# The first chunk of an input weight loaded and rounded while the batch's rows still arrive

## The chip, the cores and the metric

The kernel runs on one core of a Trainium2 chip. A core has TensorE (matrix products; the trace gives its matmuls as PE and its weight loads as PEld), VectorE (DVE), ScalarE (ACT), GpSimd (POOL) and SyncE (SP), which here issues most of the DMAs. Every engine works through its own list of instructions in order; semaphores tie the lists together. DMAs issued by SP and by ScalarE stand in two queues and share the core's 16 transfer engines. The metric is the device time of one execution in microseconds.

## The reference

```python
def _attn_ref(x):                       # x: (8, 3008, 256) f32
    X = np.fft.fft(x, axis=1)
    X = np.fft.fft(X, axis=2)
    return X.real.astype(np.float32)

def _moe_ref(x, w_in, w_out):           # (24064, 256), (256, 2048), (2048, 256)
    h = x @ w_in
    g = h * (1.0 / (1.0 + np.exp(-1.702 * h)))
    return (g @ w_out).astype(np.float32)
```

The result of the first is reshaped to 24064 rows and handed to the second. In the kernel `w_in` and `w_out` come as 64-bit floating-point values, seen as pairs of 32-bit words, and are rounded to 32 bits on the chip.

## The kernel before

The Fourier transform along the 3008 rows is split as 47 x 64. The first stage (`fold_first`, `mix_first` for batch 0; `fold1`, `mix1` for the others) combines 47 rows each, the second (`stage2`) 64. The transform along the 256 columns is folded into `w_in`: `fold_w(n)` multiplies a rounded chunk of `w_in` by cosines and sines and leaves `wcs[0]` and `wcs[1]`. So each inner step only multiplies `pq`, the result of the second stage, by `wcs`, applies the activation and multiplies by `w_out`. There are 384 steps, numbered by batch, block, half and pair. Steps 0 to 7 use plain products (`hidden(t)`, `rows(t)`, `activate(t)`, `product(t)`), while the weights are still being rounded; from step 8 on a scheme with fewer products and more sums runs, which needs differences of the rounded `w_out`.

The order of the instructions is written out by hand (`tc.manual_schedule()`), so the order of the calls is the order on each engine. The change lies in what happens before step 0, L834 to L902:

- SP loads the table `w0` in two parts (L836, L841) and batch 0's x in four pairs of row groups (`load_first(0)` to `load_first(3)`, L266, four, three, three and three DMAs). A pair holds groups `g` and `7-g` of four row slots each. Then it loads raw chunk 0 of `w_in` (`load_in(0)`, 1024 KB), the tables `small`, and raw chunk 1. At most eight of these DMAs are in flight; each semaphore is waited for before it is used again.
- `odd_weights` (L280) makes a second table from `w0` on ScalarE. `fold_first(g)` (L288, L290) folds a group on VectorE; `mix_first(i)` (L308) multiplies on TensorE and copies the result out on ScalarE (L310). After every second one `spill_first` stores the first 16 rows to `Td` in DRAM by two DMAs, one on SP's and one on ScalarE's queue (L314); the others follow later on SP. `fill` (L336) reads `Td` back as `t`, turned.
- The rounding of a raw chunk has six kinds of instruction: `squares` (L406 on ScalarE, or L408 on VectorE), `clamp` (L411, GpSimd), `low_up` (L416) and `low_down` (L421) on ScalarE, `high` (L438, L439, L440, VectorE) and `finish_in` (L452, GpSimd; `finish_out`, L460, for `w_out`), which leaves `wst`.
- `fold_w` (L182 as `psw`) takes 16 matmul passes on TensorE and two copies on ScalarE (L479). `first_row` (as `psf`) needs both copies. `rotate` (as `psr`, copy L343) and `stage2` (L356, transposes L362 on VectorE) need `t` and leave `pq`. `nyquist` (as `psn`, copy L374) makes `nb`, which `rows` needs. `warm(n)` is n matmuls without a use.

Before the change chunk 0 is rounded behind the seventh `mix_first` and later, partly in halves of 512 elements, with its squares on VectorE; `fold_w(0)`, `first_row(0)`, `rotate`, `stage2(0, 0)` follow, and `fold_w(1)` comes after `stage2`. `load_out(0)` stands on ScalarE's queue.

Of the kernel before, what the change touches and what calls it, by code (L numbers as in the profile page):

```python
# [46 lines left out]
def view(ap, offset, *dims):  # L47
    return bass.AP(ap.tensor, ap.offset + offset, [list(d) for d in dims])


def free(ap, offset, *dims):
    return bass.AP(ap.tensor, ap.offset + offset, [list(ap.ap[0])] + [list(d) for d in dims])
# [58 lines left out]
def kernel(ctx: ExitStack, tc, x, w_in, w_out, tab1, tab2, out):  # L111
    nc = tc.nc
# [43 lines left out]
    def ring(tag):  # L156
        at, size, count = rings[tag]
        i = turns[tag] = turns.get(tag, -1) + 1
        return big[:, at + i % count * size:at + (i % count + 1) * size]
# [7 lines left out]
    def bank(name, tag=None):  # L167
        if tag is None:
            tag = spare.pop(0)
            spare.append(tag)  # L170
        if tag in ("o0", "o1"):
            return o_banks[int(tag[1])]
        return (rest if tag[0] == "o" else psp).tile([128, 512], F32, tag=tag, name=name)
# [5 lines left out]
    def halves(out, lhs, rhs, **how):  # L179

        for c0 in (0, 64):
            nc.tensor.matmul(out[c0:c0 + 64], lhsT=lhs[:, c0:c0 + 64], rhs=rhs, skip_group_check=True, **how)  # L182
# [86 lines left out]
    def load_first(k):  # L269

        lo, two_ = 4 * k, (((28 - 8 * k) * D, 2), (1, 4 * D))
        load_rows(0, lo, lo, two_, two_)
        for at in lo, 28 - lo:
            skip = at == 0
            load_rows(1, at + skip, NB - at - skip, ((D, 4 - skip), (1, D)), ((-D, 4 - skip), (1, D)))
        if k == 0:
            load_rows(1, 0, NJ, ((1, D),), ((1, D),))

    def odd_weights(lo, hi):
        nc.scalar.activation(odd[:, lo:hi], w0[:, lo:hi], ACTF.Copy, scale=w0[:, n0:n0 + 1])  # L280
# [11 lines left out]
    def mix_first(i):  # L292

        ps, ns = bank("ps1"), (2 * i + 2, 2 * i + 1) if i < 7 else (0, 15)
        for at, n in enumerate(ns):
            todo = [], []
            for c, slot in enumerate((n, NJ - n if n else 16)):
                o = ps[64 * c:64 * c + 64, at * D:(at + 1) * D]
                even, odd_ = (w[:, k * NM:k * NM + 64] for w, k in ((w0, slot), (odd, slot or NJ)))
                todo[c].append((o[:, H + 1:], odd_, room[slot // 4][:, slot % 4, 0:H - 1], True, True))  # L300
                folded = slot // 4 not in BY_PE
                todo[c].append((o[:, 0:H + 1], even, xt[:, slot, 0:H + 1], True, folded))
                if not folded:
                    todo[c].append((o[:, 1:H], even, free(xt[:, slot], D - 1, [-1, H - 1]), False, True))
            for k in range(3):
                for c in range(2):
                    for o, w, rhs, first_, end in todo[c][k:k + 1]:
                        nc.tensor.matmul(o, lhsT=w, rhs=rhs, start=first_, stop=end, skip_group_check=True)  # L308
        to = 2 - i % 2 * 2
        nc.scalar.copy(made[i // 2][:, to:to + 2, :].rearrange("p j d -> p (j d)"), ps[:])  # L310
# [11 lines left out]
    def warm(n):  # L322

        ps = bank("warm")
        for _ in range(n):
            nc.tensor.matmul(ps[:], lhsT=wcs[0][:, 0:128], rhs=wcs[0][:, 0:512], start=True, stop=True)
# [59 lines left out]
    def load_in(n, eng):  # L386
        t = raw["in", n] = ring("raw").bitcast(U32).rearrange("p (n w) -> p n w", w=2)
        eng.dma_start(out=t[:].rearrange("p (i f) w -> p i (f w)", i=2),
                      in_=w_in[:, n * 512:(n + 1) * 512].bitcast(U32).rearrange("(i p) f -> p i f", p=128))

    def load_out(n, eng):
        t = raw["out", n] = ring("raw").bitcast(U32).rearrange("p (n w) -> p n w", w=2)
        eng.dma_start(out=t[:].rearrange("p (f n) w -> p f (n w)", f=4),
                      in_=w_out[4 * n * 128:(4 * n + 4) * 128, :].bitcast(U32).rearrange("(p f) n -> p f n", p=128))
# [3 lines left out]
    def prepare(key):  # L398


        pre[key] = ring("s"), ring("m"), ring("r").bitcast(U32)

    def squares(key, eng):
        g, hi = pre[key][0], raw[key][:, :, 1].bitcast(F32)
        if eng is nc.scalar:
            eng.activation(g[:], hi, ACTF.Square)  # L406
        else:
            eng.tensor_tensor(g[:], hi, hi, op=ALU.mult)  # L408

    def clamp(key, lo=0, n=1024):  # L410
        nc.gpsimd.tensor_scalar(pre[key][1][:, lo:lo + n], raw[key][:, lo:lo + n, 1].bitcast(F32), scalar1=TOP, scalar2=-TOP,  # L411
                                op0=ALU.min, op1=ALU.max)

    def low_up(key, lo=0, n=1024):

        nc.scalar.activation(pre[key][2][:, lo:lo + n].bitcast(F32), raw[key][:, lo:lo + n, 0], ACTF.Copy, scale=2.0 ** -29,  # L416
                             bias=2.0 ** 23)

    def low_down(key, lo=0, n=1024):
        r = pre[key][2][:, lo:lo + n]  # L420
        nc.scalar.activation(r, r.bitcast(F32), ACTF.Copy, bias=-2.0 ** 23)  # L421
# [8 lines left out]
    def high(key, lo=0, n=1024):  # L430

        g, m, _ = (t[:, lo:lo + n] for t in pre[key])
        bits = m.bitcast(U32)
        if lo == 0:
            made_a[key] = ring("a").bitcast(U32)
        a = made_a[key][:, lo:lo + n]
        dve = nc.vector
        dve.scalar_tensor_tensor(m, g, LOW * LOW, m, op0=ALU.is_ge, op1=ALU.mult)  # L438
        dve.tensor_scalar(a, bits, scalar1=3, scalar2=0x3FFFFFF8, op0=ALU.logical_shift_left, op1=ALU.bitwise_and)  # L439
        dve.scalar_tensor_tensor(a, bits, 0xC0000000, a, op0=ALU.bitwise_and, op1=ALU.bitwise_or)  # L440
# [5 lines left out]
    def finish_in(n, lo=0, k=1024):  # L446

        if lo == 0:
            wst[n] = op.tile([128, 2, 512], F32, tag="os", name="wst")
        key, part = ("in", n), slice(lo, lo + k)  # L450
        out = wst[n][:].rearrange("p i f -> p (i f)")[:, part]
        nc.gpsimd.tensor_tensor(out.bitcast(U32), made_a[key][:, part], pre[key][2][:, part], op=ALU.add)  # L452
# [19 lines left out]
    def fold_w(n):  # L472
        ps = [bank("psw") for _ in range(2)]
        for i in range(2):
            for cs in range(2):
                halves(ps[cs][:], cd[:, i, cs, :], wst[n][:, i, :], start=(i == 0), stop=(i == 1))
        for cs in range(2):

            nc.scalar.copy(wcs[cs][:, n * 512:(n + 1) * 512].rearrange("p (f c) -> p f c", f=4),  # L479
                           free(ps[cs][:], 0, [1, 4], [4, 128]))  # L480
# [346 lines left out]
    for i, pair_of in enumerate(((0, 7), (1, 6), (2, 5), (3, 4))):  # L827
        for k, g in enumerate(pair_of):
# [6 lines left out]
    ends = n0 + 4 - 28 * NM  # L835
    nc.sync.dma_start(out=free(w0, 0, [28 * NM, 2], [1, ends]),  # L836
                      in_=view(tab1, 0, [tab1.shape[1], 128], [28 * NM, 2], [1, ends]))
    for i in range(4):
        load_first(i)
        if i == 0:  # L840
            nc.sync.dma_start(out=w0[:, ends:28 * NM], in_=tab1[:, ends:28 * NM])  # L841
    load_in(0, nc.sync)
    nc.sync.dma_start(out=small[:], in_=tab2)
    load_in(1, nc.sync)
    odd_weights(NM, ends)
    odd_weights(28 * NM, n0)
    odd_weights(ends, 28 * NM)
    warm(6)

    in0, in1, out0, in2 = ("in", 0), ("in", 1), ("out", 0), ("in", 2)  # L850
    prepare(in0)
    for i, need in enumerate(((0, 7), (1,), (6,), (2,), (5,), (3,), (4,), ())):
        for g in need:
            fold_first(g)
        mix_first(i)
        if i % 2:
            spill_first(i // 2, 0, 16, (nc.sync, nc.scalar))
        if i == 6:
            low_up(in0, 0, 512)
            low_down(in0, 0, 512)  # L860
            squares(in0, nc.vector)
            for h0 in (0, 512):
                clamp(in0, h0, 512)
            for h0 in (0, 512):
                high(in0, h0, 512)
    load_out(0, nc.scalar)
    low_up(in0, 512, 512)
    low_down(in0, 512, 512)
    fill(0, 0, 4)
    load_in(2, nc.sync)  # L870
    for k in range(4):
        spill_first(k, 16, NM, (nc.sync, nc.sync))
    prepare(in1)
    squares(in1, nc.scalar)
    finish_in(0, 0, 512)
    clamp(in1)
    finish_in(0, 512, 512)
    low_up(in1)
    low_down(in1)
    for h0 in (0, 512):  # L880
        high(in1, h0, 512)
    load_out(1, nc.sync)
    fill(0, 4, NG)
    warm(1)
    fold_w(0)
    warm(1)
    first_row(0)
    prepare(out0)
    for h0 in (0, 512):
        finish_in(1, h0, 512)  # L890
    clamp(out0)
    rotate(0, 0, 4, nc.scalar.copy)
    squares(out0, nc.scalar)
# [4 lines left out]
    high(out0)  # L898
    load_in(3, nc.sync)
    prepare(in2)  # L900
    fold_w(1)
    finish_out(0)  # L902

    extra, early = {}, {}
# [166 lines left out]
```

## Time and profile before

| | |
|---|---|
| time, median of 4 runs | 1861.51 us (1860.86 to 1862.45) |
| profiled execution | 1860.86 us, its span 1859.1 us |
| busy in the span | PE 1840.7, PEld 1400.9, DVE 1519.7, ACT 1145.2, POOL 964.2 us |
| mean granted clock of TensorE | 0.997 |
| SP issues raw chunk 0 / chunk 1 | 13.62 / 15.09 us |
| last `mix_first` copied out | 22.44 + 0.57 us |
| `fold_w(0)`, `stage2(0, 0)`, `fold_w(1)` begin on TensorE | 26.43, 33.68, 35.83 us |
| `hidden(0)` begins | 39.31 us |

An "idle before, releaser" in brackets is the time that the engine stood still before that instruction, and what ended it. A wait for several semaphores is put down to the last. The chain of waits follows the work that ended last back to the start. The table of stretches gives each engine's busy time in chosen parts of the span, then the granted clock as a share of the full one, the transfer engines' busy share and what they moved.

### The profile page before, as it was taken

The page shows a single profiled execution, that of the slowest core. Times are in us where ns is not written, and L with a number is a line of the kernel's source. Part 1 is how long each engine was busy: PE and PEld are TensorE (multiplying, and loading weights), DVE is VectorE, ACT ScalarE, POOL GpSimd, SP SyncE. Part 2 cuts the span into 40 slices and gives each one's busy share as a digit, 9 for nine tenths or more (in the row PEclk, how much of TensorE's full clock was granted, in tenths as well). Part 3 has the DMA queues.
Part 4 walks back from the last instruction along what each step waited for, and adds up shares of the span by engine and source line. Part 5 has one row for each costly group of instructions (what it writes and reads, how often), then busy time and mean ns, then how long its engine had stood idle before and what let it go on. Part 6 is the DMA issues. An engine that isn't in the chain of part 4 may idle for free.

```text
span 1859.1 us, 56025 instructions
## 1 busy us (share of the span) xinstructions
PE 1840.7 (99%) x23700; PEld 1400.9 (75%) x23700; DVE 1519.7 (82%) x2222; ACT 1145.2 (62%) x2239; POOL 964.2 (52%) x1048
## 2 busy tenths in 40 slices
PE   8999999999999999999999999999999999999998
PEld 4577777777777777777777777777777777778776
DVE  6888788888788877987789878888888888878874
ACT  5656665666666556666665666656666666656663
POOL 3676345844367443773348643486445754434442
PEclk9999999999999999999999999999999999999999
DMA  9721340225112240113302232031411111100111
GB/s 320 162 60 35 78 74 19 65 54 98 23 30 60 62 89 19 52 45 88 63 13 57 52 86 52 17 77 34 101 31 25 36 46 36 31 18 13 22 20 24
DMA packets 150315, 106.36 MB, mean 57 GB/s; under 512 B 106041, under 2 KB 131161, under 8 KB 149488
## 3 DMA queue, kind: packets, MB, share of 16 engines
q1 hardware_dynamic: 148704, 101.20, 23.8%
q8 instruction: 187, 3.06, 0.7%
q10 hardware_dynamic: 1360, 1.57, 0.3%
q14 instruction: 64, 0.52, 0.1%
HBM read 65.46 MB, written 48.05 MB: 61 GB/s over the span
## 4 chain that ended last, share of the span: by engine, by line
PE 91%; DVE 2%; DMA 2%; POOL 2%; ACT 1%; issue 1%; SPq 0%; DVEq 0%; POOLq 0%; ACTq 0%
PE x L182 33%; PE o L182 25%; PE low L669 24%; PE o L669 4%; PE ps L253 2%; PE ps L356 1%; ACT x L576 1%; POOL big L606 0%; POOL big L607 0%; DMA big<-in_moe_w_in_dram 0%; DVE big L635 0%; PE po L182 0%; DMA t<-Td 0%; DVE big L549 0%; DMA xt<-in_x_dram 0%
## 5 line engine op out<-in xcount | busy, mean ns | idle before, releaser
L606 POOL TENSOR_TENSOR big<-big 128x256 f32<-128x256 f32 (+1 forms) x376 | 347.9, 925 | 829.3 <-ACT big L598 711.2
L182 PE MATMUL x<-pq,wcs 128*64 128x256 f32 (+1 forms) x6016 | 771.3, 377 | 1.3 <-ACT x L576 0.5
L635 DVE TENSOR_TENSOR big<-big 128x512 f32<-128x512 f32 (+1 forms) x736 | 624.7, 863 | 30.6 <-PE low L669 14.4
L182 PE MATMUL o<-big,wo 128*64 128x256 f32 (+1 forms) x4800 | 621.1, 375 | 0.0
L182 PEld LDWEIGHTS x<-pq,wcs 128*64 128x64 f32 x6016 | 410.3, 137 | 190.8 <-issue 15.0
L182 PEld LDWEIGHTS o<-big,wo 128*64 128x64 f32 x4800 | 342.2, 137 | 147.1 <-DVE big L613 0.5
L588 ACT ACTIVATE g<-x 128x512 f32<-128x512 f32 (+1 forms) x376 | 221.6, 589 | 375.2 <-PE x L182 374.1
L549 DVE TENSOR_TENSOR big<-g,x 128x512 f32<-128x512 f32 (+2 forms) x440 | 253.7, 588 | 197.5 <-ACT big L591 197.1
L669 PE MATMUL low<-big 128*64 128x128 f32 (+1 forms) x5888 | 382.8, 270 | 0.0
L576 ACT ACTIVATE x<-nb,af 128x256 f32<-128x256 f32 (+1 forms) x752 | 352.8, 469 | 12.2
L669 PEld LDWEIGHTS low<-big 128*64 128x64 f32 x5888 | 337.6, 137 | 29.2
L607 POOL TENSOR_TENSOR big<-big 128x256 f32<-128x256 f32 (+1 forms) x376 | 358.7, 954 | 0.0
L591 ACT ACTIVATE big<-x 128x512 f32<-128x512 f32 (+1 forms) x376 | 220.4, 586 | 196.2 <-PE x L182 165.5
L598 ACT ACTIVATE big<-big 128x512 f32<-128x512 f32 (+1 forms) x376 | 231.9, 617 | 40.0 <-DVE big L549 38.0
L669 PE MATMUL low<-big,wo 128*64 128x128 f32 (+1 forms) x2944 | 220.2, 270 | 0.1
L669 PEld LDWEIGHTS low<-big,wo 128*64 128x64 f32 x2944 | 171.6, 137 | 3.2 <-DVE big L635 0.4
L614 DVE TENSOR_TENSOR big<-big 128x512 f32<-128x512 f32 (+1 forms) x188 | 157.6, 839 | 6.5
L613 DVE TENSOR_TENSOR big<-big 128x512 f32<-128x512 f32 (+1 forms) x188 | 136.8, 728 | 5.5 <-POOL big L606 5.5
L770 DVE TENSOR_TENSOR big<-big,low 128x512 f32<-128x512 f32 (+3 forms) x184 | 109.1, 610 | 3.5
L669 PEld LDWEIGHTS o<-big,wo 128*64 128x64 f32 x1472 | 92.3, 137 | 24.9
L669 PE MATMUL o<-big,wo 128*64 128x128 f32 (+1 forms) x1472 | 110.0, 270 | 0.0
L225 POOL TENSOR_TENSOR xt<-xt 111x510 f32<-111x510 f32 x56 | 82.3, 1469 | 4.4
(92 smaller groups left out, 953.4 us busy)
## 6 DMA issues: line engine op xcount, KB each, us to landing
out_dram<-os SPq DMA_DIRECT2D x284, 64.0 KB
t<-Td SPq DMA_DIRECT2D x22, 512.0 KB
Td<-xt SPq DMA_DIRECT2D x56, 192.0 KB
xt<-in_x_dram SPq DMA_DIRECT2D x18, 512.0 KB
xt<-Xr SPq DMA_DIRECT2D x14, 512.0 KB
nb<-Nd SPq DMA_DIRECT2D x23, 256.0 KB
out_dram<-os SPq DMA_DIRECT2D x96, 56.0 KB
Xr<-in_x_dram SPq DMA_DIRECT2D x7, 752.0 KB
```

Of the source, the lines that this page charges most:

```text
L182: nc.tensor.matmul(out[c0:c0 + 64], lhsT=lhs[:, c0:c0 + 64], rhs=rhs, skip_group_check=True, **how)
L549: nc.vector.tensor_tensor(free(out, at + m - 1, [by, 2], [RUN, blocks], [-1, m]), *ins, op=op)
L576: nc.scalar.activation(x[:, i * 256:i * 256 + n], nbt[b, blk][:, hh * 256:hh * 256 + n], ACTF.Copy, scale=af1[:, f:f + 1])
L588: nc.scalar.activation(two(g[:], n), two(xb[t][:], n), ACTF.Copy, scale=2.0)
L591: nc.scalar.activation(front(t), two(xb[t][:], width(t)), ACTF.Gelu_apprx_sigmoid)
L598: nc.scalar.activation(back(t), back(t), ACTF.Gelu_apprx_sigmoid)
L606: eng.tensor_tensor(right(t, S1, n), left(t, A21, n), right(t, A22, n), op=ALU.add)
L607: eng.tensor_tensor(left(t, S3, n), left(t, A11, n), left(t, A21, n), op=ALU.subtract)
L613: eng.tensor_tensor(s2, s1, a11, op=ALU.subtract)
L614: eng.tensor_tensor(s4, a12, s2, op=ALU.subtract)
L635: nc.vector.tensor_tensor(out, i0, i1, op=how)
L669: nc.tensor.matmul(o, lhsT=lhs, rhs=rhs, start=first_in, stop=(p == NP - 2), skip_group_check=True)
```

## The change

Raw chunk 0 is loaded right behind x's first pair, ahead of the second part of `w0` and of x's other three pairs. Its squares, `low_up`, `low_down` (ScalarE) and `clamp` (GpSimd) are issued in one piece ahead of the last `odd_weights`; its `high` and `finish_in` stand behind the first `mix_first`. `load_out(0)` is issued by SP, behind the stores after the sixth `mix_first`. The warm-up matmul ahead of `fold_w(0)` is gone, and `fold_w(1)` comes ahead of `rotate` and `stage2(0, 0)`.

```diff
+    in0, in1, out0, in2 = ("in", 0), ("in", 1), ("out", 0), ("in", 2)
     for i in range(4):
         load_first(i)
         if i == 0:
+            load_in(0, nc.sync)
             nc.sync.dma_start(out=w0[:, ends:28 * NM], in_=tab1[:, ends:28 * NM])
-    load_in(0, nc.sync)
     nc.sync.dma_start(out=small[:], in_=tab2)
     load_in(1, nc.sync)
     odd_weights(NM, ends)
     odd_weights(28 * NM, n0)
+    prepare(in0)
+    squares(in0, nc.scalar)
+    low_up(in0)
+    low_down(in0)
+    clamp(in0)
     odd_weights(ends, 28 * NM)
     warm(6)
 
-    in0, in1, out0, in2 = ("in", 0), ("in", 1), ("out", 0), ("in", 2)
-    prepare(in0)
     for i, need in enumerate(((0, 7), (1,), (6,), (2,), (5,), (3,), (4,), ())):
         for g in need:
             fold_first(g)
         mix_first(i)
+        if i == 0:
+            high(in0)
+            for h0 in (0, 512):
+                finish_in(0, h0, 512)
         if i % 2:
             spill_first(i // 2, 0, 16, (nc.sync, nc.scalar))
-        if i == 6:
-            low_up(in0, 0, 512)
-            low_down(in0, 0, 512)
-            squares(in0, nc.vector)
-            for h0 in (0, 512):
-                clamp(in0, h0, 512)
-            for h0 in (0, 512):
-                high(in0, h0, 512)
-    load_out(0, nc.scalar)
-    low_up(in0, 512, 512)
-    low_down(in0, 512, 512)
+        if i == 5:
+            load_out(0, nc.sync)
     fill(0, 0, 4)
     load_in(2, nc.sync)
     for k in range(4):
         spill_first(k, 16, NM, (nc.sync, nc.sync))
     prepare(in1)
     squares(in1, nc.scalar)
-    finish_in(0, 0, 512)
     clamp(in1)
-    finish_in(0, 512, 512)
     low_up(in1)
     low_down(in1)
     for h0 in (0, 512):
         high(in1, h0, 512)
     load_out(1, nc.sync)
     fill(0, 4, NG)
-    warm(1)
     fold_w(0)
     warm(1)
     first_row(0)
     prepare(out0)
     for h0 in (0, 512):
         finish_in(1, h0, 512)
+    fold_w(1)
     clamp(out0)
     rotate(0, 0, 4, nc.scalar.copy)
     squares(out0, nc.scalar)
     stage2(0, 0)
...
     high(out0)
     load_in(3, nc.sync)
     prepare(in2)
-    fold_w(1)
     finish_out(0)
```

## The prediction

> **What bounds the kernel now.** I read the page first, then the timeline of the first 50 us engine by engine, then the chain of waits there, and last the table of stretches for the granted clock.
>
> The page's chain says what a change at the start can be worth:
>
> ```profile
> PE 91%; DVE 2%; DMA 2%; POOL 2%; ACT 1%; issue 1%; SPq 0%; DVEq 0%; POOLq 0%; ACTq 0%
> PE x L182 33%; PE o L182 25%; PE low L669 24%; PE o L669 4%; PE ps L253 2%; PE ps L356 1%; ACT x L576 1%; POOL big L606 0%; POOL big L607 0%; DMA big<-in_moe_w_in_dram 0%; DVE big L635 0%; PE po L182 0%; DMA t<-Td 0%; DVE big L549 0%; DMA xt<-in_x_dram 0%
> ```
>
> From about 62 us on TensorE sets the time, and the change does not touch that work. Whatever it does happens before the first inner steps; what counts is when these start, and a shift there moves the end by as much. The marker I use is VectorE's first instruction of `rows(1)`. The timeline leads up to it (start us, us, engine, line; in brackets the idle time before and its releaser):
>
> ```profile
> 11.68 0.69 DVE L288 TENSOR_TENSOR first<-xt 128x508 f32<-128x508 f32 x1 [1.00 <-DMA xt<-in_x_dram]
> 20.54 1.23 DVE L408 TENSOR_TENSOR big<-big 128x1024 f32<-128x1024 f32 x1 [1.98 <-DMA big<-in_moe_w_in_dram]
> 26.15 1.13 ACT L406 ACTIVATE big<-big 128x1024 f32<-128x1024 f32 x1
> 33.77 1.28 POOL L452 TENSOR_TENSOR wst<-big 128x512 uint32<-128x512 uint32 x1 [1.09 <-DVE big L440]
> 35.83 3.65 PE L182 MATMUL psw<-wst,small 128*64 128x512 f32 x16
> 39.31 1.03 PE L182 MATMUL pa<-pq,wcs 128*64 128x256 f32 x8
> 42.26 0.59 ACT L374 COPY nb<-psn 128x512 f32<-128x512 f32 x1 [1.28 <-PE psn L182]
> 45.96 0.57 ACT L520 COPY v<-pa 128x512 f32<-128x512 f32 x1
> 46.55 0.69 DVE L558 TENSOR_TENSOR big<-v,pb 128x512 f32<-128x512 f32 x1 [2.07 <-ACT v L520]
> ```
>
> Read upward: 46.55 waited for ScalarE's copy, that for the rounding of chunk 2 behind the copy of `nb` at 42.26, that for TensorE: `hidden(0)` at 39.31 plus two 1.0 us groups. `hidden(0)` stood behind the second transform (35.83), whose operand GpSimd finished at 33.77 + 1.28 = 35.05. So before, both raw chunks, loaded after x, are rounded between 20.54 and 35.05, and this serial work sets the pace.
>
> The chain shows the price of a store on ScalarE's queue with and without SP's loads in flight:
>
> ```profile
> 17.90 6.06 DMA Td<-big
> 24.03 2.19 DMA Td<-e
> ```
>
> The table of stretches (busy us per engine, then granted clock, DMA share, GB/s) shows the clock and the loads:
>
> ```profile
> 9.36:12.77 3.41, 1.90 (x20) 1.14 (x18) 2.35 (x5) 1.78 (x2) 0.00 (x0) 1.00 1.03 386
> 12.77:16.19 3.42, 3.14 (x30) 3.05 (x30) 3.31 (x6) 0.58 (x1) 0.00 (x0) 0.50 1.06 380
> 23.01:26.43 3.42, 0.00 (x0) 0.00 (x1) 3.32 (x5) 1.49 (x4) 1.63 (x2) 1.00 0.80 199
> 26.43:29.84 3.41, 3.41 (x8) 0.76 (x8) 3.34 (x4) 2.94 (x3) 2.70 (x2) 0.50 0.93 353
> ```
>
> The loads run at 380 to 400 GB/s without a gap until about 24 us. TensorE is granted half its clock in the stretch after one in which it was idle, or busy for 1.90 of 3.41 us.
>
> **The change part by part.** Times are of the profiled execution (span 1859.1, 1.8 around it, 1860.86 in all, 0.65 under the median 1861.51).
>
> *Chunk 0 loaded behind x's first pair.* 1024 KB ahead of the rest of `w0` and x's other three pairs: at 380 to 400 GB/s 2.6 to 2.8 us. The fold that started at 11.68 has its data at 14.4. The load is moved past 10 DMAs on SP's queue (the rest of `w0`, nine of x); they wait for it in the transfer engines, and the total up to chunk 1 is the same bytes, so `small` and chunk 1 land as before (chunk 1 about 25.2: ScalarE and GpSimd use it at 26.15 and 26.35 with no wait of theirs for it).
>
> *Chunk 0 rounded while x arrives.* It lands near 10.7 (the first fold ran at 7.95, then 1024 KB). ScalarE: three passes of 1024 elements as in the rows of chunk 1, 1.13 + 1.14 + 1.06, until 14.1; ScalarE has only the 1.20 us `odd_weights` to do behind it, before its first copies. GpSimd's clamp 1.30, until 12.1. VectorE's three instructions cost 1.18 + 0.69 + 1.23 = 3.1 (rows at 36.25 to 39.4), so 12.1 to 15.3. Their cover is the wait for x, now 2.7 longer; it ends at 14.4, so 0.9 shows. GpSimd's two adds (1.57 each) are done by 18.5, beside the folds. What goes in exchange: the squares on VectorE (1.23 at 20.54), twelve half-size instructions on VectorE and GpSimd, four on ScalarE, all between 20.5 and 30.
>
> *First stage of batch 0.* VectorE's folds took 11.68 to 18.56 in one piece; now 15.3 to 22.2, x's pairs coming at the same 2.7 us. TensorE ended 3.15 behind them (21.71) because it ran at half clock to 16.19. In the later start the half-clock stretch falls on the first folds, and it has two groups of about 0.9 left after the last fold: 24.0 to 25.3, I take 24.2. Bounds: no shift beyond x's 2.7, or the old lag in full.
>
> *First transform straight behind it.* No warm-up matmul, no wait for GpSimd: 16 matmuls, 3.45, 24.2 to 27.7. But its copies (L479) stand on ScalarE behind chunk 1's three passes, and `warm(1)` and `first_row(0)` wait for these copies.
>
> *Chunk 1 on ScalarE.* Ahead of it stands the last store on ScalarE's queue, which waits for the second one's landing. The second was issued at 17.90; now 3.1 later, at 21.0. With loads in flight it takes up to 6.06, without 2.19: 23.2 to 27.1. Before it landed with the loads of the time, so I take 26.1, near the upper row. L406 then starts at 26.4 (before 26.15), the passes end at 29.7. Chunk 1's own landing bounds it below at 25.3.
>
> [...]
>
> *Chunk 1 on VectorE and GpSimd.* Before, it waited for chunk 0 until 28.13. Now it starts at 27.6: first half 0.68 + 0.43 + 0.69, second 0.68 + 1.38 + 0.69 (the 1.38 is the row beside a running GpSimd, 0.43 that without); GpSimd's halves at 29.7 and 32.2, done at 33.8, 1.25 earlier than before.
>
> *Second transform, now ahead of `rotate` and stage 2.* TensorE: copy L479 done at 30.3 and 30.9, warm-up, `psf` to 31.9. At full clock it needs 1.72 per half, the second half from 33.8: end 35.5. TensorE is idle from 27.7 to 30.3, in a stretch that may grant half afterwards; half clock over one stretch of 3.4 ends it at 37.0. The start of the kernel shifts against these stretches, so I take the middle, 36.3.
>
> [...]
>
> *Stage 2.* It comes after the transform instead of before it. `rotate`'s copy now stands behind two L479 on ScalarE: 0.7 + 0.2. Then the second half of stage 2 (0.6), and the transposes (1.44), which were hidden under the second transform and now stand bare: `hidden(0)` at 36.3 + 2.9 = 39.2, against 39.31. `high(out0)` moves behind the transposes, 39.4 to 42.5, and `rows(0)` with it to 42.6; its row had 2.07 of idle time after it, which covers this. `finish_out(0)` ends near 45, before the first product (49.78).
>
> *`load_out(0)` on SP instead of ScalarE.* It stands ahead of the last store of the first 16 rows on SP, and takes 2.7. That store lands near 29.4 instead of 25 to 26, and the first read of `t` (26.37 before, used at 33.47 without a wait, so at most 7.1 long) is issued at 29.5 and is there between 33 and 36.5. Stage 2 wants it at 36.3: hidden, with nothing to spare at the upper end. ScalarE's queue loses 0.49 of issuing.
>
> *Sum.* The operand of the second transform: chunk 1's start +0.25, one chunk less in VectorE's and GpSimd's way -1.5, so 33.8 for 35.05. From there to `hidden(0)` it was 4.26; now it is 1.72 + 0.8 for the clock + 2.9 = 5.4, so +1.15. Together -0.1: median 1861.51 - 0.1 = 1861.4.
>
> **The rivals.** *Faster:* the store lands before chunk 1 (L406 at 25.4), GpSimd does not slow VectorE, TensorE stays at full clock: the transform runs through from 30.9 to 34.4, `hidden(0)` at 36.95, 2.35 earlier: 1859.2. For it: each row exists at the low value. Against: all three are needed.
>
> *Slower:* ScalarE's store waits out the whole SP queue, which now holds `load_out(0)` too. Its bytes are in at 27.2; with 2.19 the second store lands at 29.4, L406 starts at 29.75, 3.35 later than in my sum, and the longer gap on TensorE (27.7 to 33.5) puts the whole first half of the transform at half clock: 36.3 becomes 40.4, and the time 1865.5. It decides from a landing at about 29. For it: 6.06. Against: SP issues that load only near 23.3, 2.3 after the store.
>
> *Hidden:* the shift is absorbed where the chain touches GpSimd, between 107 and 125 us (`big`, `xt`): 1861.5 whatever happens before. Against: VectorE has no idle time in its rows from 46.55 to 64, TensorE works on from there, and GpSimd waits for their results.
>
> *The change does not do what it says* if chunk 0 lands after x's second pair; against that is the queue order, which has it behind 1.3 MB only.
>
> **How the numbers follow.** About 0.2% (3.7 us) is what a measurement of this kernel can tell from no change. My case (within 1.5 of the median): 0.5. Faster rival and what lies towards it: 0.2, of which 0.06 goes under -3.7 (something that I have as serial is not). Slower rival and towards it: 0.25, of which 0.16 reaches +3.7 (the store, a late `t`, or the clock on top). Hidden: 0.05. So faster 0.06, same 0.78, slower 0.16. Range: 1858.8 (under the faster rival) to 1865.6 (the slower one), leaving out about 2 in 10.
>
> **What would show it.** Right: VectorE's `high` of chunk 0 between two folds near 12 to 15; first stage ending near 24; L406 of chunk 1 near 26.4; last L452 of chunk 1 near 33.8; `hidden(0)` at 39 +- 1; `rows(1)` at 46.5. Wrong: L406 after 28 (store), a stretch at 0.50 around 31 to 37 longer than one (clock), `psr` waiting for `t` (read), or folds slowed beside GpSimd's adds.

## The result and the profile after

The changed kernel takes 1865.09 us (median of 38 runs, 1863.58 to 1866.73) against 1861.43 for the kernel before (58 runs on the same chips, 1860.72 to 1864.01). The ratio is 1.0018, 95% interval 1.0014 to 1.0023: slower by 3.66 us. I forecast no change, 1861.4. The profiled execution of the changed kernel took 1864.27, its span is 1862.4 (before 1859.1).

The chain of the page looks as before, with TensorE in nearly all of it (92% for 91%). So the place to look is again the start. The timeline of the changed kernel (start us, us, engine, line, operation; in brackets the idle time before and its releaser), the lines that answer to those of before, and the folds; other rows are left out:

```profile
11.65 1.13 ACT L406 ACTIVATE big<-big 128x1024 f32<-128x1024 f32 x1 [7.11 <-DMA big<-in_moe_w_in_dram]
...
12.89 1.23 DVE L438 SCALAR_TENSOR_TENSOR big<-big 128x1024 f32<-128x1024 f32 x1 [2.16 <-POOL big L411]
...
16.02 0.68 DVE L288 TENSOR_TENSOR first<-xt 128x508 f32<-128x508 f32 x1
16.26 3.23 POOL L452 TENSOR_TENSOR wst<-big 128x512 uint32<-128x512 uint32 x2 [3.45 <-DVE big L440]
16.73 1.63 DVE L290 TENSOR_TENSOR xt<-xt 128x508 f32<-128x508 f32 x1
18.29 1.75 DVE L288 TENSOR_TENSOR first<-xt 128x508 f32<-128x508 f32 x1
20.07 0.69 DVE L290 TENSOR_TENSOR xt<-xt 128x508 f32<-128x508 f32 x1
...
23.32 1.28 DVE L288 TENSOR_TENSOR big<-xt 128x508 f32<-128x508 f32 x2
...
28.95 1.17 ACT L406 ACTIVATE big<-big 128x1024 f32<-128x1024 f32 x1 [0.44 <-ACT e L310]
...
34.91 1.27 POOL L452 TENSOR_TENSOR wst<-big 128x512 uint32<-128x512 uint32 x1 [1.09 <-DVE big L440]
...
34.42 3.75 PE L182 MATMUL psw<-wst,small 128*64 128x512 f32 x16
...
40.84 1.08 PE L182 MATMUL pa<-pq,wcs 128*64 128x256 f32 x8 [0.20 <-DVE pq L362]
...
48.14 0.69 DVE L558 TENSOR_TENSOR big<-v,pb 128x512 f32<-128x512 f32 x1 [1.82 <-ACT v L520]
...
67.92 1.08 PE L182 MATMUL pb<-pq,wcs 128*64 128x256 f32 x8 [0.50 <-DVE t L343]
...
1237.36 0.29 PE L253 MATMUL ps<-e,w 47*64 47x129 f32 x1 [0.50 <-DVE big L549]
```

Chunk 0 lands at 11.65 and is rounded before the second pair of x is folded, as the change says. Then two folds that take 0.69 alone take 1.63 and 1.75 while GpSimd makes chunk 0's two adds (16.26 to 19.49). The last fold ends at 24.60 (before 18.56). ScalarE's squares of chunk 1 start at 28.95 (before 26.15), the last add of chunk 1 ends at 36.18 (before 35.05), `hidden(0)` starts at 40.84 (before 39.31), `rows(1)` at 48.14 (before 46.55). So 1.59 us are lost when the inner steps start. The line at 67.92 is a second loss: a `pb` matmul waits 0.50 us for VectorE's copy L343. The line at 1237.36 is a third: TensorE waits 0.50 us for VectorE in the first stage of a later batch. Before, the rows that answer to these two stand without a bracket:

```profile
65.65 1.03 PE L182 MATMUL pb<-pq,wcs 128*64 128x256 f32 x8
...
66.10 0.16 DVE L343 COPY t<-psr 128x8 f32<-128x8 f32 x1
...
1234.78 0.32 PE L253 MATMUL ps<-e,w 47*64 47x129 f32 x1
```

There `pb` started 0.45 ahead of that copy. After it the changed kernel is 2.3 us behind instead of 1.6. Near 920 us it wins back 0.3, and at the wait of 1237.36 it loses 0.7, which makes 2.7 up to TensorE's last matmul; the rest of the 3.3 between the spans lies behind that. The wait at 1237 us stands in the traces of all four kernels that keep `high(in0)` behind the first `mix_first` (the changed one and three of those below) and in none of the other nine traces. What ties it to that place is not shown.

The chain of waits of the changed kernel (start us, us, what; steps of issuing are left out) names the work that sets the end of the first part:

```profile
16.73 1.65 DVE xt L290
18.42 9.47 PE ps L308 x122
27.92 0.59 ACT e L310
28.54 0.36 ACTq L314
28.95 1.17 ACT big L406
```

It runs from the slowed fold through TensorE's first stage, then ScalarE's last copy, the issue of the store, and the squares of chunk 1. The store is issued without a wait; what holds the squares is the first stage. In the same kernel's stretches (busy us of PE, PEld, DVE, ACT, POOL, with instructions, then granted clock, DMA share, GB/s):

```profile
12.77:16.19 3.42, 0.00 (x0) 0.00 (x0) 3.23 (x4) 3.39 (x5) 0.04 (x1) 0.50 1.07 389
16.19:19.60 3.41, 1.87 (x16) 1.47 (x17) 3.38 (x3) 0.26 (x1) 3.23 (x2) 0.50 1.07 380
19.60:23.01 3.41, 3.41 (x32) 2.91 (x30) 3.31 (x6) 1.17 (x2) 0.00 (x0) 0.53 1.03 411
...
29.84:33.25 3.41, 1.92 (x9) 0.66 (x6) 2.93 (x5) 3.37 (x5) 0.89 (x1) 1.00 0.45 183
33.25:36.66 3.41, 3.41 (x28) 1.22 (x28) 1.54 (x2) 0.24 (x2) 2.32 (x3) 1.00 0.71 226
```

TensorE is idle in the first of them and at half clock for nearly all of the first three, so the first stage has two suspects: the folds and the clock. In the second transform (34.42) the clock is full (1.00).

### The profile page after: what moved, and what is told of

The parts are those of the page before. It is cut to its first block, busy times and chain, and to the rows that moved or that the text cites. A ratio compares the mean times of both kernels' runs of the same rounds, so it can differ in the third digit from the quotient of the medians.

```text
span 1862.4 us, 56008 instructions
## 1 busy us (share of the span) xinstructions
PE 1839.3 (99%) x23698; PEld 1401.5 (75%) x23698; DVE 1516.9 (81%) x2218; ACT 1145.5 (62%) x2238; POOL 961.9 (52%) x1047
## 4 chain that ended last, share of the span: by engine, by line
PE 92%; DVE 3%; ACT 2%; issue 1%; POOL 1%; DMA 0%; SPq 0%; ACTq 0%; DVEq 0%; POOLq 0%
PE x L182 34%; PE o L182 25%; PE low L669 24%; PE o L669 4%; PE ps L253 2%; PE ps L356 1%; DVE big L635 1%; PE ps L308 1%; ACT x L576 0%; DVE big L549 0%; DMA big<-in_moe_w_in_dram 0%; PE psw L182 0%; DVE big L770 0%; PE po L182 0%; DVE big L438 0%
## 5 line engine op out<-in xcount | busy, mean ns | idle before, releaser
L606 POOL TENSOR_TENSOR big<-big 128x256 f32<-128x256 f32 (+1 forms) x376 | 348.1, 926 | 829.9 <-ACT big L598 704.4
```

The costliest lines, as they stand in the source:

```text
L606: eng.tensor_tensor(right(t, S1, n), left(t, A21, n), right(t, A22, n), op=ALU.add)
```

## The experiments

Theory A: the delay at the start comes from the folds, which start late behind `high(in0)` and which GpSimd's adds slow by 2.0 us (0.94 and 1.07 in the two rows above). Theory B: it comes from TensorE's half clock. Theory C, for the wait at 67.92: one of the two warm-ups is gone, and with it one turn of the six rotating PSUM banks (`spare`, which `bank()` takes from the front and puts back at the end), so that every later tile sits in the next bank and one of them meets a reader that is not done. Times are compared with the kernel before on the same chip (1861.2 to 1861.3).

**The bank alone, in the changed kernel.** One turn of the banks is put in the place of the removed warm-up.

```diff
+    spare.append(spare.pop(0))
     fold_w(0)
```

> The changed kernel with the PSUM banks turned on by one place ahead of fold_w(0), as the removed warm-up matmul did; no instruction is added. Bank theory: the matmul group pb of hidden(5) no longer waits for VectorE's copy of rotate (0.50 of PE idle at 67.92 in the changed kernel), the step from +1.59 to +2.32 us between 65 and 70 us goes, and the time falls by 0.7 to about 1864.4. Rival, that this step belongs to the loads of batch 1 or to the later start: no change, 1865.1.

Measured: 1863.98, ratio 1.0012 [1.0003, 1.0021], with `hidden(0)` at 40.68 and `rows(1)` at 47.97. The timeline of this kernel has the same `pb` without a wait:

```profile
67.08 1.03 PE L182 MATMUL pb<-pq,wcs 128*64 128x256 f32 x8
...
67.52 0.16 DVE L343 COPY t<-psr 128x8 f32<-128x8 f32 x1
```

It starts ahead of the copy again. The distance to the trace of before stays at 1.4 between 60 and 75 us, where the changed kernel goes from 1.6 to 2.3. C holds, and the delay at the start is untouched by it.

**The bank alone, in the kernel before.** The same warm-up is taken out there, nothing else.

```diff
-    warm(1)
     fold_w(0)
```

> The kernel before with the warm-up matmul ahead of fold_w(0) taken out and nothing else. Bank theory: TensorE's pb of hidden(5) waits for VectorE's copy of rotate as in the changed kernel, a step of +0.7 us between 65 and 70 us, 1862.1. Rival, that the banks only matter with the later start: no change, 1861.4.

Measured: 1862.44, ratio 1.0006 [0.9997, 1.0015]. The time alone would not decide; the timeline does:

```profile
66.28 1.08 PE L182 MATMUL pb<-pq,wcs 128*64 128x256 f32 x8 [0.51 <-DVE t L343]
66.05 0.16 DVE L343 COPY t<-psr 128x8 f32<-128x8 f32 x1
```

`rows(1)` is at 46.44, 0.11 earlier than before, and after this `pb` the kernel is 0.67 behind. So the wait needs no early load; dropping the warm-up makes it.

**Chunk 0's adds out of the folds' way.** In the changed kernel the two adds of GpSimd go behind the clamp of chunk 1.

```diff
         if i == 0:
             high(in0)
-            for h0 in (0, 512):
-                finish_in(0, h0, 512)
...
     clamp(in1)
+    for h0 in (0, 512):
+        finish_in(0, h0, 512)
```

> The changed kernel with GpSimd's two adds of chunk 0 put behind the clamp of chunk 1, so that GpSimd stands still while VectorE folds. Theory that the adds slow the folds: the two folds that took 1.63 and 1.75 take 0.69, the folds end about 2.0 earlier (22.6), the first stage ends 1.3 to 2.0 earlier than 27.9; fold_w(0) then begins near 29.4, and hidden(0) gains less than 1 us, 1864.3 to 1865.1. Rival, that these folds are slow by the transfers or by late data: they stay at 1.6 and 1.7 us, and the first stage still ends at 27.9.

Measured: 1862.56, ratio 1.0007 [0.9998, 1.0016], so 2.5 less than the changed kernel. Its timeline shows the folds:

```profile
16.23 0.69 DVE L290 TENSOR_TENSOR xt<-xt 128x508 f32<-128x508 f32 x1
16.84 0.68 DVE L288 TENSOR_TENSOR first<-xt 128x508 f32<-128x508 f32 x1
...
20.80 1.28 DVE L288 TENSOR_TENSOR big<-xt 128x508 f32<-128x508 f32 x2
```

They take 0.69 each and end at 22.08 instead of 24.60; 0.5 of these 2.5 us come from chunk 0, which landed at 11.15 in this execution for 11.65. `rows(1)` is at 46.90. The first stage, though, ends at 26.64, 4.56 behind the last fold, not 3.2: its stretch before 16.19 is idle and the two after it are granted 0.50 and 0.59. With the folds mended, the clock is what is late next, by some 1.3 us. So A holds for the adds; the time fell by more than the 0.8 at most that I had expected.

**The clock alone.** Nine warm-up matmuls behind the first group of the changed kernel are to keep TensorE busy in its gap; five turns more bring the banks back to where they were (nine matmuls take one tile).

```diff
         mix_first(i)
         if i == 0:
+            warm(9)
+            for _ in range(5):
+                spare.append(spare.pop(0))
```

> The changed kernel with nine warm-up matmuls behind the first mix_first, in TensorE's gap of 12 to 16.7 us, the banks left as in the changed kernel. Clock theory: TensorE is granted the full clock from about 16 us instead of 22.8, follows the folds by less than 2 us instead of 3.3, the first stage ends at 26.5 instead of 27.9, chunk 1's squares begin at 27.5 instead of 28.95, and the time is 1.4 lower, 1863.7. Rival, that the folds alone set the end of the first stage: it ends within 0.4 of 27.9 and the time stays at 1865.1.

Measured: 1864.90, ratio 1.0021 [1.0012, 1.0030], no gain. One stretch of this kernel, and TensorE's rows at its two ends:

```profile
16.19:19.60 3.41, 3.41 (x9) 1.52 (x8) 3.38 (x3) 0.12 (x1) 3.12 (x2) 1.00 1.07 377
12.35 7.99 PE L326 MATMUL warm<-wcs 128*128 128x512 f32 x18
20.40 0.44 PE L308 MATMUL ps<-first,wo 128*64 128x127 f32 x4
```

The clock is full from 12.77 to 23.01 (granted 1.00 in each stretch), the folds end at 24.42 and the first stage at 27.65, 3.23 behind them. But the nine matmuls run as 18 passes until 20.34, well past the gap: the second group starts at 20.40 instead of 16.76, though its fold was done at 18.19. So this run alone does not tell what a full clock is worth; it may have lost to the warm-ups what it won by the clock. The rows of the two kernels do tell it (before, then changed; the fold of the changed one is above, at 23.32):

```profile
17.22 1.34 DVE L288 TENSOR_TENSOR big<-xt 128x508 f32<-128x508 f32 x2
18.05 0.29 PE L308 MATMUL ps<-big,wo 128*64 128x127 f32 x1
24.15 0.29 PE L308 MATMUL ps<-big,wo 128*64 128x127 f32 x1
```

TensorE takes up the first matmul that reads a `big` fold 0.83 us after that fold starts, in both kernels. So in the changed kernel it had made up for its half clock by then, and the folds alone set the end of the first stage: B falls there. From that matmul to the end the last three groups take 3.73 us in both (18.05 to 21.78, 24.15 to 27.88), so the 3.2 us behind the last fold are work. With the adds late the same matmul comes 2.14 after its fold (22.94 for 20.80): there the clock is late by 1.3.

**Rounding of chunk 0 behind the folds.** The early load stays, as do ScalarE's passes and the clamp; VectorE's `high(in0)` and GpSimd's adds come at the seventh group, when the folds are done.

```diff
-        if i == 0:
+        if i == 6:
             high(in0)
```

> The changed kernel with high and finish_in of chunk 0 behind the seventh mix_first, as before the change, but loaded early and with ScalarE's passes and the clamp early. Theory that VectorE's three instructions and the adds hold up the folds: the fold of x's second pair begins at 14.9 instead of 16.0, all of them take 0.69 and end near 22, and the first stage ends near 25; chunk 0's adds then end at 28.4 and hold the clamp of chunk 1, so of the 3 us some 0.7 are left at hidden(0): 1864.4. Rival, that x coming 2.7 us later decides alone: the first stage ends at 27 or later and the time is 1865.1 or more.

Measured: 1861.81, ratio 1.0002 [0.9993, 1.0011]. The second pair's fold starts at 14.69 (wait for x) instead of 16.02, the folds end at 21.63 and the first stage at 24.82. TensorE resumes 1.3 earlier (15.43 for 16.76), and its half clock ends in the stretch to 19.60 (granted 0.61, then 1.00). `hidden(0)` is at 39.20 and `rows(1)` at 46.52, where they were before; the bank step then brings 0.7, as in the changed kernel. The time is 2.6 below the 1864.4 that I had expected, since `hidden(0)` loses nothing.

**Both repairs.** The same with the turn of the banks.

```diff
-        if i == 0:
+        if i == 6:
             high(in0)
...
+    spare.append(spare.pop(0))
     fold_w(0)
```

> The changed kernel with both suspects out at once: high and finish_in of chunk 0 behind the seventh mix_first, and the banks turned on by one place ahead of fold_w(0). If these two account for the whole loss: no step between 65 and 70 us, rows(1) at 46.5, time within 0.5 of the kernel before, 1861.2. If something third is left: 1862 or more.

Measured: 1861.14, ratio 0.9998 [0.9989, 1.0007]. `rows(1)` is at 46.57, and the distance to before stays under 0.1 past 70 us. With both causes out, the loss is gone from the time. The two account for 2.3 us in the marks up to 75 us and for some 4 in the median; of the rest, 0.7 is the wait at 1237 us, which is gone too, and where the remainder sat is not located.

**The second transform early, alone.** The kernel before with `fold_w(1)` ahead of `rotate` and stage 2.

```diff
     for h0 in (0, 512):
         finish_in(1, h0, 512)
+    fold_w(1)
     clamp(out0)
...
-    fold_w(1)
     finish_out(0)
```

> The kernel before with fold_w(1) ahead of rotate and stage2 and nothing else. Theory that the transposes then stand bare and rotate's copy waits behind two copies: the second transform ends near 36.8 instead of 39.5, hidden(0) follows 2.7 to 2.9 after it, 39.6 against 39.31, and the time is 0 to +0.6, 1861.4 to 1862.0. Rival, that fold_w(1) out of the way of hidden(0) is a gain by itself: hidden(0) at 38.5 or earlier, 1860.6.

Measured: 1862.05, ratio 1.0005 [0.9996, 1.0014]. `psw` runs from 34.08 to 37.73 and `hidden(0)` comes at 40.41, 2.68 behind it: the transposes lie bare, as I had priced them. `rows(1)` is 1.16 late, but 1.4 of lateness was there before: in this execution the folds ended at 19.13 (before 18.56) and the first stage at 23.15 (before 21.78), with half clock from 11.8 to 18.6 instead of one stretch (granted 0.86, 0.50 and 0.64 in the stretches from 9.36 on). Counted from chunk 1's last add (35.65) it is 4.76 to `hidden(0)`, where it was 4.26 before. So a gain from the new order by itself is not seen, and what it costs in the time is not settled.

**`load_out(0)` on SP, alone.** In the kernel before it goes where the changed kernel has it.

```diff
+        if i == 5:
+            load_out(0, nc.sync)
...
-    load_out(0, nc.scalar)
```

> The kernel before with load_out(0) issued by SP behind the stores after the sixth mix_first and nothing else. Theory that it holds up the last store and so the read of t: the read is issued near 29.5 instead of 26.37, t is there near 33 to 34.5, psr waits up to 1 us for it, and the time is +0.3 to +1.0. Rival, that t has slack: hidden(0) within 0.2 of 39.3 and the time unchanged, 1861.4.

Measured: 1861.96, ratio 1.0003 [0.9994, 1.0012]. `psr` starts at 34.52 right behind TensorE's work ahead of it, without a wait for `t`. `rows(1)` is 1.04 late, behind a first stage that ended 1.95 late: x's second pair came 1.0 later in this execution (the fold starts at 12.72 for 11.68), and the half clock lasted two stretches (granted 0.50 and 0.53). For the time it is inconclusive; for `t` it agrees with my step.

**What the early load can give.** The kernel before with the early load and chunk 0's first passes, its `high` and adds in one piece behind the folds, the second transform and the warm-ups where they were, and `load_out(0)` on SP behind the first read of `t`.

```diff
         if i == 0:
+            load_in(0, nc.sync)
...
+    prepare(in0)
+    squares(in0, nc.scalar)
+    low_up(in0)
+    low_down(in0)
+    clamp(in0)
     odd_weights(ends, 28 * NM)
...
         if i == 6:
...
+            high(in0)
+            for h0 in (0, 512):
+                finish_in(0, h0, 512)
+        if i % 2:
+            spill_first(i // 2, 0, 16, (nc.sync, nc.scalar))
-    load_out(0, nc.scalar)
...
     fill(0, 0, 4)
+    load_out(0, nc.sync)
```

> The kernel before with chunk 0 loaded behind x's first pair, its passes on ScalarE and the clamp early, high and finish_in in one piece behind the seventh mix_first, load_out(0) on SP behind the first read of t; the warm-up matmul and the place of fold_w(1) as before. If the early load is worth something by itself once VectorE's folds are left alone: first stage ends near 24.9, stage2 by 33, the second transform starts at 34, hidden(0) at 37.6 to 38.5, time 0.8 to 1.7 under the kernel before, 1859.7 to 1860.6. If x's 2.7 us eat it: hidden(0) at 39.3 or later and 1861.4 or more.

Measured: 1860.44, ratio 0.9995 [0.9986, 1.0004]. `hidden(0)` is at 38.04 and `rows(1)` at 45.29, 1.27 earlier than before. Its timeline names what is late now:

```profile
28.50 0.69 DVE L438 SCALAR_TENSOR_TENSOR big<-big 128x512 f32<-128x512 f32 x1 [3.83 <-POOL big L411]
...
32.20 0.28 PE L182 MATMUL psr<-t,small 128*64 128x4 f32 x4 [0.46 <-DMA t<-Td]
```

VectorE waits 3.83 for chunk 1's clamp, which stands on GpSimd behind chunk 0's adds. A second set of runs of the same kernel:

> The early load with the folds left alone, the same kernel as run before, to narrow its interval: 0.7 to 1.5 below the kernel before, as measured once (1860.44 against 1861.19) and as its profile has it (rows(1) at 45.29 against 46.55). Rival, that the gain was chance: no difference.

Measured: 1859.75, ratio 0.9993 [0.9985, 1.0002], `hidden(0)` at 37.62, `rows(1)` at 44.87. The gain is seen in both, and neither interval shuts out 1.

**The best version.** Two edits to that kernel: the adds of chunk 0 behind the clamp of chunk 1, and the warm-up behind `stage2(0, 0)` exchanged for a turn of the banks.

```diff
             high(in0)
-            for h0 in (0, 512):
-                finish_in(0, h0, 512)
...
     clamp(in1)
+    for h0 in (0, 512):
+        finish_in(0, h0, 512)
...
     stage2(0, 0)
-    warm(1)
+    spare.append(spare.pop(0))
```

> The same, but with chunk 1's clamp ahead of chunk 0's adds on GpSimd, and the warm-up matmul behind stage2 replaced by a turn of the banks. If the second transform there waits for the warm-up and for the second add (34.46 in the run with the early load): it starts at 33.6, ends near 37.1, hidden(0) at 37.0 against 38.04, time 1.0 lower, 1859.4. Rival, that TensorE loses the clock or that fold_w(0), whose operand comes 1.4 later, holds up the rest: hidden(0) at 38 or later, 1860.4 or more.

Measured: 1858.93, ratio 0.9986 [0.9977, 0.9995], so faster than the kernel before by some 2.4 us and than the changed one by 6. Its timeline:

```profile
25.22 2.53 POOL L452 TENSOR_TENSOR wst<-big 128x512 uint32<-128x512 uint32 x2
...
26.57 1.72 DVE L438 SCALAR_TENSOR_TENSOR big<-big 128x512 f32<-128x512 f32 x1 [2.40 <-POOL wst L452]
...
36.54 1.03 PE L182 MATMUL pa<-pq,wcs 128*64 128x256 f32 x8
...
43.81 0.69 DVE L558 TENSOR_TENSOR big<-v,pb 128x512 f32<-128x512 f32 x1 [2.10 <-PE pb L182]
```

`hidden(0)` stands at 36.54, `rows(1)` at 43.81, 2.75 earlier than before, and the span is 1856.4. GpSimd's adds still slow a VectorE instruction (1.72 for 0.69), but that one is not in the chain of the first stage.

## Why the prediction was wrong

**"GpSimd's two adds (1.57 each) are done by 18.5, beside the folds" — the step that failed first.** I gave it no cost, though I named folds slowed beside these adds among the signs of being wrong. It cost 2.0 us on VectorE, in the chain that sets the end. A row of before would have shown it. These are from VectorE's and GpSimd's timeline of the kernel before:

```profile
87.89 0.95 DVE L679 TENSOR_TENSOR big<-wo 128x256 f32<-128x256 f32 x1
...
90.23 0.41 DVE L679 TENSOR_TENSOR big<-wo 128x256 f32<-128x256 f32 x1
...
91.02 0.92 DVE L679 TENSOR_TENSOR big<-wo 128x256 f32<-128x256 f32 x1
86.77 3.53 POOL L470 TENSOR_TENSOR wo<-wo 128x256 f32<-128x256 f32 x4
```

The same line takes 0.41 once L470 is done (90.30) and 0.92 to 0.95 in these rows while it or a GpSimd add such as L606 runs; one row beside a later L470, at 94.72, keeps 0.42. I had seen such a slowing, 1.38 for 0.43, and applied it to chunk 1's rounding, but not to the folds. In the changed kernel each slowed fold ended about 0.55 us behind the end of one add (18.36 and 20.04, the adds ending near 17.8 and at 19.49), and the two adds together took 3.23 where they take 2.50 with VectorE idle (the run with the rounding behind the folds). So both engines lost time there; by what means they slow each other, no run here shows.

**"12.1 to 15.3 … so 0.9 shows" for `high(in0)`.** Chunk 0 landed at 11.65 and not near 10.7; `high` ended at 16.1, and the fold of the second pair began at 16.02 for the 15.3 of my sum. With 8.58 us for the folds in place of 6.88, that makes the 24.60 for 22.2. (The half-size instructions that the prediction counts as twelve are ten in the rows; the sum does not use them.)

**"The first stage ending near 24" (24.2, bounds 24.0 to 25.3).** It ended at 27.88, 3.28 behind the last fold. I had put the 3.15 of before down to the half clock, and let it shrink. The rows speak against it: from the first matmul on the last folds (18.05, in a stretch granted 1.00) the three groups left took 3.73, before as after, so the lag is work. The old lag in full was the right end of my bounds, on a fold end 2.4 too early. The clock does count where the folds are not late, as the run with late adds shows (granted 0.50 and 0.59, the first stage 4.56 behind the last fold).

**"L406 near 26.4".** It was 28.95. The slower rival had the place right (after 28) and the mechanism wrong: it had the second store's landing hold ScalarE's queue, and the chain shows a store issued without a wait behind the first stage's last copies. My warning sign "L406 after 28 (store)" would therefore have pointed to the wrong cause. That this rival's 1865.5 lies near the measured 1865.09 is luck.

**From the second transform's operand to `hidden(0)`.** The last add ended at 36.18 for 33.8, so 2.4 late, and from there on it was 4.66 for my 5.4: the 0.8 for the clock did not come, and the transposes lay bare at 2.7 for my 2.9. `t` was there: `psr` started at 38.00 with no wait. In all `hidden(0)` came at 40.84 for 39.2.

**"No warm-up matmul" — missed altogether.** I booked the removed `warm(1)` as a gain of its time. It was also one turn of the banks, and that cost 0.7 us some 40 us later, past the point where I had stopped following the change. No rival of mine held it.

**Right** were the early rounding itself, chunk 1's landing, `t`, the price of the bare transposes, and that a shift of the inner steps' start reaches the end. In the sum, the term for the operand was mis-sized (36.18 for 33.8), the term behind it was 0.7 too large, and a term of 0.7 was missing; 2.3 of the 3.66 us are so accounted for in the marks. Another 0.7 is the wait at 1237 us, of which the prediction had nothing and whose cause stays open.

## What to carry to other kernels

Before work is called hidden beside another engine's, look for a row where the same kind of instruction runs beside that other engine and one where it runs alone: here VectorE's folds took 1.63 and 1.75 us beside GpSimd's adds and 0.69 alone. A removed instruction that took a tile from a rotating set moves every later tile by one: keep the turn, and look for new waits far behind the edit (here 0.50 us at 67.92). When two suppliers of one stage are late by nearly the same amount, mending one of them shows less than its full size: with the adds late the folds ended 2.5 us earlier and the first stage only 1.2. And a filler that is put on an engine to keep its clock up takes the engine's time as well (here until 20.34, with the next fold done at 18.19): see that it ends before the work behind it is ready, or the run tests the filler.

## What had not been expected of the hardware

In these traces the half clock does not follow from a stretch's busy share alone. Before, the stretch from 9.36 to 12.77 was busy for 1.90 us and the next was granted 0.50. In the changed kernel the stretch from 29.84 to 33.25 was busy for 1.92 and the next was granted 1.00. So the price I set for such a gap was drawn from one sample of two; what else the grant goes by, no run here shows.

The clock's history and the arrival of x also differ between executions of nearly the same code: the first stage ended at 21.78 in the kernel before, and at 23.15 and 23.73 in two runs that left its start alone. There the half clock lasted two stretches instead of one, and the last folds ended 0.57 and 0.93 later. A single trace's end of the first stage is therefore good to about 2 us in that order, and these two runs of a single part stay open for that reason.
